# A fused attention and two-layer MLP kernel: block 1 from f32 to three f16 passes, with the elementwise work dealt out anew among VectorE, ScalarE and GpSimd

## The chip, the cores and the metric

One core of a Trainium2 chip. The metric is the device time of one execution in microseconds (us), the median of several executions; lower is better. The engines are named PE (TensorE), DVE (VectorE), ACT (ScalarE), POOL (GpSimd) and SP (SyncE, which issues the DMAs here).

## The reference

Inputs are f32 for q, k, v, p and f64 bits for the weights, decoded to f32 on the chip. Sizes: 8 batches, 8 heads, 576 tokens each, head size 64, 32 packed rows; 4608 tokens in all.

```python
def sm_attn(qq, kk, vv):            # softmax(qq kk^T / 8) vv
    ...
p_packed = sm_attn(p, k, v)         # 32 rows per head
x = sm_attn(q, p_packed, p_packed)  # (4608, 512) after the heads are joined
# first layer: d_ff 2048
h = x @ w_in
P = a[0] + a[1]*h + a[2]*h**2 + a[3]*h**3
Q = 1.0 + abs(b[0])*abs(h) + abs(b[1])*h**2
x = (P / (Q + 1e-06)) @ w_out
# second layer: d_ff 1024
h = x @ w_in2
solu = h * softmax(h)
ln = (solu - mean(solu)) / sqrt(var(solu) + 1e-06) * g_ln
out = ln @ w_out2
```

## The kernel before

Tokens go through in 9 blocks (index j) of 512. `attention(b)` makes the packed rows of batch b: scores (`a_s1`), transposes (`a_tr`), product with v (`a_pp`), a transpose and a maximum (`a_pt`), and `a_pw`, which multiplies the packed rows by `w_in`, so that the first layer's matmul takes the attention weights of a block straight to h. `a_s2` makes the attention weights of block j on DVE (a chain of 1024-column instructions) into the tile `at`.

A block has 16 tiles i of 128 rows of d_ff by 512 tokens. `m_h` makes h of one tile on PE; `elem` turns it into the ratio g; `m_y` multiplies g by four slices of `w_out` and adds into four PSUM banks. After tile 15, `y_out` copies the sum to `ybig`, and the second layer follows in four groups of 128 tokens: `s_h2` (PE), `s_sm` (maximum, exp, product), `s_lt` (halves and a DMA transpose into `lbig`), `s_ln` (a chain of small POOL instructions) and `s_out` (PE, then a copy and the output DMA).

A matmul is either f32, or three f16 passes of operands split into a high and a low half (high by high, high by low, low by high). `NRAW` says how many leading blocks and batches stay f32: with `NRAW = 2`, blocks 0 and 1 have f32 g and f32 `w_out` in `m_y`, and batches 0 and 1 have f32 `pw` and f32 attention weights in `m_h`. From then on `w_split(1, c)` has replaced chunk c of f32 `w_out` (w2) by its two halves, in place and one slot further down, so that split c+1 overwrites the slot that split c read. Splitting needs a scale (`wst`, from the maximum over all of that weight); `a_pw` halves need `bnd` (from a bound over the columns of `w_in`), and the scaled coefficients of `elem` need the chain `a_scale` (tile `cf`, some 27 small steps, and `asc` for the attention weights).

`elem` of one tile before: ACT takes |h| to u; POOL makes s = (b1 u + b0) u in two instructions (L691 through the helper at L335, and L692); ACT and DVE make the numerator B; ACT takes 1/Q as exp(-ln) (L696, L697); DVE makes one correction step and the product (L698, L699, L701 or L703); from block 2 on ACT casts the high half of g (L704) and POOL subtracts for the low half (L705). u, s and B have three buffers each, h two PSUM banks, g three.

At the start all weights are loaded and decoded by DVE (`w_decode`, L399 to L401, 24 groups of 256 rows by 512 or so), through stages that lie in the places of later weights.

The order on each engine is fixed ahead by `Plan.order`: a list scheduler with a cost in ns for each part, which takes for a free engine the ready part with the smallest due time. A due time is 16 j + an offset from the table `DUE` (one for each kind of part, or one for (block, kind)) + the tile's index; a part isn't taken while its due time is more than `DUE["ahead"]` beyond PE's present tile. Each engine then runs its list in order and waits on semaphores.

## Time and profile before

| | |
|---|---|
| median of 3 executions | 1197.74 us (1196.11 to 1203.66) |
| the profiled execution, its own time | 1202.27 us |
| its span, first to last instruction | 1200.4 us |
| PE busy | 1115.8 us, 93% |
| DVE busy | 976.8 us, 81% |
| ACT busy | 762.0 us, 63% |
| POOL busy | 706.3 us, 59% |

The span is cut by the copies that end each block's sum (L728). Block 0's begins at 194.6 us, block 1's at 327.3, block 2's at 450.0 and block 8's at 1148.8; times within the span are in us from its start. A busy share is the union of an engine's instructions; PE's contains the filling and draining of its pipeline.

### The profile page before, as it was taken

The page shows a single profiled execution, that of the slowest core. Times are in us where ns is not written, and L with a number is a line of the kernel's source. Part 1 is how long each engine was busy: PE and PEld are TensorE (multiplying, and loading weights), DVE is VectorE, ACT ScalarE, POOL GpSimd, SP SyncE. Part 2 cuts the span into 40 slices and gives each one's busy share as a digit, 9 for nine tenths or more (in the row PEclk, how much of TensorE's full clock was granted, in tenths as well). Part 3 has the DMA queues.
Part 4 walks back from the last instruction along what each step waited for, and adds up shares of the span by engine and source line. Part 5 has one row for each costly group of instructions (what it writes and reads, how often), then busy time and mean ns, then how long its engine had stood idle before and what let it go on. Part 6 is the DMA issues. An engine that isn't in the chain of part 4 may idle for free.

```text
span 1200.4 us, 17951 instructions
## 1 busy us (share of the span) xinstructions
PE 1115.8 (93%) x6549; PEld 529.7 (44%) x6550; DVE 976.8 (81%) x1477; ACT 762.0 (63%) x1256; POOL 706.3 (59%) x931
## 2 busy tenths in 40 slices
PE   4678989999999999999999998999999999999998
PEld 1133344444444454444544454444444444444443
DVE  5987999999978978888878887888788886788633
ACT  3556666676856667567756766577656666667624
POOL 0163847554658647676666655765675865867612
PEclk9698999999999999999999999999999999999999
DMA  9664033110222121311231114111311121211123
GB/s 342 224 230 161 7 123 99 36 53 1 54 77 67 27 54 55 88 27 28 62 109 27 27 40 131 27 27 27 117 28 27 27 53 28 53 27 27 27 53 88
DMA packets 108120, 83.54 MB, mean 70 GB/s; under 512 B 78208, under 2 KB 88576, under 8 KB 108032
## 3 DMA queue, kind: packets, MB, share of 16 engines
q1 hardware_dynamic: 108032, 82.40, 24.4%
q8 instruction: 51, 0.84, 0.3%
q14 instruction: 37, 0.30, 0.1%
HBM read 54.07 MB, written 9.44 MB: 53 GB/s over the span
## 4 chain that ended last, share of the span: by engine, by line
PE 47%; DVE 23%; POOL 13%; ACT 9%; issue 5%; DMA 2%; SPq 0%; DVEq 0%; ACTq 0%; POOLq 0%
PE P L329 37%; PE h L329 9%; POOL s L692 4%; POOL cf L335 3%; DVE B L699 3%; POOL s L335 2%; DVE s L698 2%; POOL g L705 2%; ACT u L696 2%; DVE B L694 2%; DVE B L695 2%; POOL d L335 1%; DVE w L401 1%; DMA lbig<-lbig 1%; DVE at L629 1%
## 5 line engine op out<-in xcount | busy, mean ns | idle before, releaser
L329 PE MATMUL P<-g,w 128*128 128x512 f16 (+1 forms) x1600 | 423.4, 414 | 0.7 <-DVE ybig L729 0.7
L329 PE MATMUL h<-at,pw 128*128 128x192 f16 (+11 forms) x1408 | 235.4, 315 | 8.3 <-ACT at L646 3.2
L335 POOL TENSOR_SCALAR s<-u,aba 128x512 f32<-128x512 f32 x130 | 137.6, 1058 | 173.7 <-ACT u L690 150.9
L329 PEld LDWEIGHTS <-w 128*128 128x128 f16 x1440 | 138.4, 98 | 167.5 <-issue 12.1
L329 PE MATMUL P<-w,ybig 128*128 128x512 f16 x864 | 193.9, 381 | 9.0 <-DVE pw L539 2.5
L705 POOL TENSOR_TENSOR g<-B,g 128x512 f16<-128x512 f32 x112 | 144.2, 1287 | 80.9 <-ACT g L704 76.6
L692 POOL TENSOR_TENSOR s<-s,u 128x512 f32<-128x512 f32 x130 | 186.3, 1433 | 7.0
L329 PE MATMUL P<-w,lbig 128*128 128x512 f16 x768 | 173.0, 379 | 4.9 <-DVE pw L539 2.9
L335 POOL TENSOR_SCALAR d<-d 128x1 f32<-128x1 f32 x216 | 85.3, 395 | 156.6 <-ACT E L790 73.1
L696 ACT ACTIVATE u<-s,lnb 128x512 f32<-128x512 f32 x130 | 93.8, 721 | 98.4 <-POOL s L692 97.9
L698 DVE SCALAR_TENSOR_TENSOR s<-s,u 128x512 f32<-128x512 f32 x130 | 109.2, 840 | 47.8 <-ACT u L697 47.0
L329 PEld LDWEIGHTS <-ybig 128*128 128x128 f16 x864 | 84.7, 98 | 114.2 <-issue 16.0
L329 PEld LDWEIGHTS <-pw 128*128 128x128 f16 x1152 | 101.6, 98 | 64.5 <-issue 13.3
L329 PEld LDWEIGHTS <-lbig 128*128 128x128 f16 x768 | 74.6, 98 | 92.6 <-issue 8.1
L694 DVE SCALAR_TENSOR_TENSOR B<-h,cf,B 128x512 f32<-128x512 f32 x112 | 83.0, 741 | 27.5 <-ACT B L693 27.3
L693 ACT ACTIVATE B<-h,cf 128x512 f32<-128x512 f32 x112 | 86.6, 773 | 21.5 <-POOL g L705 21.5
L699 DVE SCALAR_TENSOR_TENSOR B<-B,cf,u 128x512 f32<-128x512 f32 x101 | 98.2, 972 | 0.0
L697 ACT ACTIVATE u<-u,lnb 128x512 f32<-128x512 f32 x133 | 95.6, 719 | 2.0
L690 ACT ACTIVATE u<-h,cf 128x512 f32<-128x512 f32 x101 | 68.9, 682 | 39.9 <-PE h L329 38.1
L695 DVE SCALAR_TENSOR_TENSOR B<-B,cf,h 128x512 f32<-128x512 f32 x112 | 82.8, 739 | 1.5
L704 ACT CAST g<-B 128x512 f16<-128x512 f32 x112 | 68.6, 613 | 21.6 <-PE P L329 16.9
L703 DVE SCALAR_TENSOR_TENSOR B<-s,B 128x512 f32<-128x512 f32 x98 | 81.0, 827 | 1.1
(144 smaller groups left out, 1469.3 us busy)
## 6 DMA issues: line engine op xcount, KB each, us to landing
w<-in_w_in_dram SPq DMA_DIRECT2D x10, 1024.0 KB, 9.2
kq<-in_kT_dram SPq DMA_DIRECT2D x8, 1152.0 KB, 6.2
w<-in_w_out_dram SPq DMA_DIRECT2D x9, 1024.0 KB, 8.1
kq<-in_qT_dram SPq DMA_DIRECT2D x9, 1024.0 KB, 5.4
out_dram<-w SPq DMA_DIRECT2D x36, 256.0 KB, 2.4
v<-in_vN_dram SPq DMA_DIRECT2D x15, 512.0 KB, 3.7
lbig<-in_w_out_dram SPq DMA_DIRECT2D x3, 1024.0 KB, 5.4
lbig<-in_w_in_dram SPq DMA_DIRECT2D x2, 1024.0 KB, 7.0
```

What stands on the lines that cost most here:

```text
L329: nc.tensor.matmul(out=o, lhsT=lhsT, rhs=rhs, start=start, stop=stop)
L335: gp.tensor_scalar(out=o, in0=i, scalar1=s1, scalar2=s2, op0=o0, **({"op1": o1} if o1 else {}))
L692: pool(due, c_pool(512, 2), lambda: gp.tensor_tensor(out=T(s_), in0=T(s_), in1=T(u_), op=ALU.mult), [u_, s_], [s_])
L693: sc(due, c_act(512, 163), lambda: act.activation(out=T(B_), in_=T(h_), func=AF.Identity, scale=coef(17), bias=coef(16)), [h_, *R], [B_], ...
L694: dve(due, c_dve(512), lambda: stt(out=T(B_), in0=T(h_), scalar=coef(14), in1=T(B_), op0=ALU.mult, op1=ALU.mult), [h_, B_, *R], [B_])
L695: dve(due, c_dve(512), lambda: stt(out=T(B_), in0=T(B_), scalar=coef(15), in1=T(h_), op0=ALU.subtract, op1=ALU.mult), [h_, B_, *R], [B_])
L696: sc(due, c_act(512, 105), lambda: act.activation(out=T(u_), in_=T(s_), func=AF.Ln, scale=2.0 ** -40, bias=lnb[:, 0:1]), [s_, "lnb"], [u_])
L697: sc(due, c_act(512, 105), lambda: act.activation(out=T(u_), in_=T(u_), func=AF.Exp, scale=-1.0, bias=lnb[:, 1:2]), [u_, "lnb"], [u_])
L698: dve(due, c_dve(512, 140), lambda: stt(out=T(s_), in0=T(s_), scalar=1.0 + 1e-6, in1=T(u_), op0=ALU.add, op1=ALU.mult), [s_, u_], [s_])
L699: dve(due, c_dve(512, 240), lambda: stt(out=T(B_), in0=T(B_), scalar=coef(18), in1=T(u_), op0=ALU.subtract, op1=ALU.mult), [B_, u_, *R], [B_])
L703: dve(due, c_dve(512, 95), lambda: stt(out=T(B_), in0=T(s_), scalar=2.0, in1=T(B_), op0=ALU.subtract, op1=ALU.mult), [s_, B_], [B_])
L705: pool(due, (1250, 1290), lambda: gp.tensor_tensor(out=T(g_)[:, 1, :], in0=T(B_), in1=T(g_)[:, 0, :], op=ALU.subtract), [B_, g_], [g_])
```

## The change

- `NRAW` goes from 2 to 1: block 1 takes g and `w_out` as f16 halves, and batch 1 takes `pw` and attention weights as f16 halves (448 of block 1's 512 tokens and 128 of block 2's; the 64 tokens of batch 0 in block 1 stay f32). `w_split(1, c)` now stands among block 0's tiles.
- For `w_out`, the low half no longer comes from one DVE instruction: ACT scales the f32 chunk in place, and POOL subtracts the high half.
- In block 0, and on the even tiles of later blocks, s comes from ACT (Square, and Abs with a new coefficient) and one DVE instruction; POOL keeps the odd tiles of blocks 1 to 8.
- `a_scale` has one more small POOL step.
- The planner gets other costs, a rule that it starts no part marked `port` while another such part or a POOL part is under way in its model, and a new table of due times, with offsets for each weight group and for blocks 0, 1 and 8.

```diff
-    NRAW = 2
+    NRAW = 1
+    LOW_POOL = {1: 1, 2: 0, 3: 0}
+    Q_POOL = lambda j, i: j > 0 and i % 2
+    LO_POOL = lambda j, i: True
...
+        if port or eng == "POOL":
+            self.port.add(n)
...
+                        if n in self.port and port_at > now:
+                            held.append((due, n))
+                            continue
...
+                    if got in self.port:
+                        port_at = now + occ
...
-        lat = (2.4 * n + 220) if tensors > 1 else (1.3 * n + 330)
+        lat = (2.14 * n + 175) if tensors > 1 else (0.94 * n + 290)
...
+        if LOW_POOL[w]:
+            sc(due, c_act(512, 100), lambda: act.activation(out=raw[w][:, c + 1, :], in_=raw[w][:, c + 1, :], func=AF.Copy, scale=s), [b, ("wst", w), a], [b])
+            pool(due, (1117, 1157), lambda: gp.tensor_tensor(out=spl[w][:, c, 1, :], in0=raw[w][:, c + 1, :], in1=spl[w][:, c, 0, :], op=ALU.subtract), [a, b], [a, ("spl", w, c)])
+            return
...
+                      ("p", C(22), C(14), abc[:, 4:5], None, ALU.mult),
...
-        sc(due, c_act(512, 65), lambda: act.activation(out=T(u_), in_=T(h_), func=AF.Abs, scale=coef(14)), [h_, *R], [u_], [(u_, "u"), (s_, "s")])
-        pool(due, c_pool(512), lambda: ps_(T(s_), T(u_), aba[:, 5:6], aba[:, 4:5], ALU.mult, ALU.add), [u_, "ab"], [s_])
-        pool(due, c_pool(512, 2), lambda: gp.tensor_tensor(out=T(s_), in0=T(s_), in1=T(u_), op=ALU.mult), [u_, s_], [s_])
+        if Q_POOL(j, i):
+            sc(due, c_act(512, 65), lambda: act.activation(out=T(u_), in_=T(h_), func=AF.Abs, scale=coef(14)), [h_, *R], [u_], [(u_, "u"), (s_, "s")])
+            pool(due, c_pool(512), lambda: ps_(T(s_), T(u_), aba[:, 5:6], aba[:, 4:5], ALU.mult, ALU.add), [u_, "ab"], [s_])
+            pool(due, c_pool(512, 2), lambda: gp.tensor_tensor(out=T(s_), in0=T(s_), in1=T(u_), op=ALU.mult), [u_, s_], [s_])
+        else:
+            sc(due, c_act(512, 65), lambda: act.activation(out=T(s_), in_=T(h_), func=AF.Square, scale=coef(14)), [h_, *R], [s_], [(s_, "s")])
+            sc(due, c_act(512, 65), lambda: act.activation(out=T(u_), in_=T(h_), func=AF.Abs, scale=coef(22)), [h_, *R], [u_], [(u_, "u")])
+            dve(due, c_dve(512), lambda: stt(out=T(s_), in0=T(s_), scalar=aba[:, 5:6], in1=T(u_), op0=ALU.mult, op1=ALU.add), [u_, s_, "ab"], [s_], port=True)
...
```

## Rows read from the trace of the kernel before

**Rows 1.** The page's first part: busy time of each engine in us (its share of the span) and its instructions.

```profile
PE 1115.8 (93%) x6549; PEld 529.7 (44%) x6550; DVE 976.8 (81%) x1477; ACT 762.0 (63%) x1256; POOL 706.3 (59%) x931
```

**Rows 2.** Busy time by stretches: the stretch, its length, then busy us (instructions) of PE, PEld, DVE, ACT, POOL, the granted share of PE's clock, the DMA engines' share, GB/s.

```profile
0.00:60.00 60.00, 31.28 (x245) 11.59 (x249) 45.69 (x64) 27.96 (x56) 5.07 (x8) 0.80 0.80 283
60.00:83.60 23.60, 23.14 (x115) 9.22 (x108) 20.77 (x31) 16.28 (x29) 13.27 (x6) 1.00 0.79 292
83.60:93.10 9.50, 0.00 (x0) 0.01 (x1) 4.73 (x6) 3.40 (x6) 5.95 (x2) 0.67 0.00 0
93.10:194.60 101.50, 94.44 (x494) 40.09 (x494) 93.82 (x148) 64.06 (x119) 59.72 (x67) 0.96 0.32 104
194.60:327.30 132.70, 129.14 (x512) 61.01 (x511) 127.52 (x195) 93.92 (x158) 73.90 (x92) 1.00 0.15 41
327.30:450.00 122.70, 118.85 (x782) 59.53 (x781) 101.09 (x154) 78.63 (x126) 78.86 (x109) 1.00 0.23 55
450.00:1148.80 698.80, 671.03 (x4190) 326.78 (x4189) 563.16 (x845) 456.36 (x735) 461.17 (x617) 1.00 0.19 48
```

**Rows 3.** The page's chain of work that ended last, its shares of the span by engine.

```profile
PE 47%; DVE 23%; POOL 13%; ACT 9%; issue 5%; DMA 2%; SPq 0%; DVEq 0%; ACTq 0%; POOLq 0%
```

**Rows 4.** PE's instructions grouped by line, tiles and shape over the span: count, busy us, mean ns of one record, idle before. An f32 matmul leaves two records, an f16 pass one.

```profile
L329 PE MATMUL P<-g,w 128*128 128x512 f16 x1344 | 307.8, 379 | 0.2 <-DVE ybig L729 0.2
...
L329 PE MATMUL P<-g,w 128*128 128x512 f32 x256 | 115.7, 598 | 0.5 <-DVE ybig L729 0.5
...
L329 PE MATMUL h<-at,pw 128*128 128x448 f32 x64 | 27.6, 553 | 0.0
...
L329 PE MATMUL h<-at,pw 128*128 128x448 f16 x96 | 20.8, 353 | 0.4 <-DVE B L695 0.4
...
L329 PE MATMUL h<-at,pw 128*128 128x128 f32 x64 | 10.1, 281 | 0.0
...
L329 PE MATMUL h<-at,pw 128*128 128x128 f16 x96 | 8.0, 219 | 0.0
```

**Rows 5.** Instructions in order of time around 83 us, from POOL's, PE's and DVE's timelines: start, us, engine, line, operation, tiles, count, and idle time before it with what ended it.

```profile
77.41 10.88 POOL L335 TENSOR_SCALAR s<-u,aba 128x512 f32<-128x512 f32 x1 [3.73 <-DVE g L701]
...
93.13 0.59 PE L329 MATMUL P<-w,ones 128*32 128x512 bf16 x1 [9.54 <-ACT pw L534]
...
77.16 1.21 DVE L401 SCALAR_TENSOR_TENSOR w<-w,w 128x1024 uint32<-128x1024 uint32 x1
...
96.35 0.28 DVE L332 TENSOR_SCALAR p<-P,sum 128x64 f32<-128x64 f32 x1 [8.02 <-PE P L329]
```

**Rows 6.** DVE's groups between 60 and 450 us: count, busy us, mean ns, idle before.

```profile
L698 DVE SCALAR_TENSOR_TENSOR s<-s,u 128x512 f32<-128x512 f32 x50 | 37.6, 753 | 5.1 <-ACT u L697 4.9
L699 DVE SCALAR_TENSOR_TENSOR B<-B,abc,u 128x512 f32<-128x512 f32 x32 | 29.1, 910 | 0.0
L458 DVE SCALAR_TENSOR_TENSOR w<-w,wst 128x512 f16<-128x512 f32 x32 | 26.8, 843 | 0.0
...
L699 DVE SCALAR_TENSOR_TENSOR B<-B,cf,u 128x512 f32<-128x512 f32 x18 | 17.9, 995 | 0.0
L703 DVE SCALAR_TENSOR_TENSOR B<-s,B 128x512 f32<-128x512 f32 x18 | 16.1, 893 | 0.2
...
L539 DVE SCALAR_TENSOR_TENSOR pw<-P,bnd,pw 128x1024 f16<-128x1024 f32 x8 | 10.2, 1276 | 1.7 <-ACT pw L538 1.7
```

**Rows 7.** Three DVE lines over the span: count, duration of one in ns (least/median/most), first and last start. h lies in PSUM; s, u and B lie in SBUF.

```profile
L698 DVE SCALAR_TENSOR_TENSOR s<-s,u x130: 643/692/3035, 64.3 to 1133.6; 128x512 f32<-128x512 f32 x130
...
L694 DVE SCALAR_TENSOR_TENSOR B<-h,cf,B x112: 707/740/753, 303.3 to 1136.2; 128x512 f32<-128x512 f32 x112
...
L699 DVE SCALAR_TENSOR_TENSOR B<-B,cf,u x101: 734/746/1760, 305.4 to 1139.3; 128x512 f32<-128x512 f32 x101
```

**Rows 8.** POOL's groups between 60 and 450 us, the same columns as rows 6.

```profile
L692 POOL TENSOR_TENSOR s<-s,u 128x512 f32<-128x512 f32 x50 | 75.0, 1499 | 3.2
L335 POOL TENSOR_SCALAR s<-u,aba 128x512 f32<-128x512 f32 x49 | 65.3, 1332 | 80.3 <-ACT u L690 59.5 <-DVE g L701 18.6 <-ACT d L793 1.3
L705 POOL TENSOR_TENSOR g<-B,g 128x512 f16<-128x512 f32 x18 | 23.3, 1297 | 12.1 <-ACT g L704 12.0
```

**Rows 9.** ACT's groups between 60 and 450 us, the same columns.

```profile
L457 ACT ACTIVATE w<-w,wst 128x512 f16<-128x512 f32 x32 | 22.7, 715 | 10.2 <-DVE w L458 5.1 <-DVE w L452 3.9 <-POOL wst L335 1.1
...
L690 ACT ACTIVATE u<-h,cf 128x512 f32<-128x512 f32 x19 | 12.9, 680 | 4.6 <-PE h L329 4.5
L704 ACT CAST g<-B 128x512 f16<-128x512 f32 x18 | 11.0, 610 | 3.7 <-DVE B L703 2.5 <-PE P L329 1.2
```

**Rows 10.** In order of time: the first and last part of block 0's `cf` chain on POOL, the copy that ends block 1's attention weights on ACT, and the first h matmuls of block 1 on PE.

```profile
122.72 0.92 POOL L335 TENSOR_SCALAR cf<-pmx 128x1 f32<-128x1 f32 x2
...
134.15 1.59 POOL L335 TENSOR_SCALAR cf<-cf 128x1 f32<-128x1 f32 x2
...
138.51 1.12 ACT L646 COPY at<-E 128x128 f32<-128x128 f32 x2
...
156.38 2.12 PE L329 MATMUL h<-at,pw 128*128 128x64 f32 x8
```

**Rows 11.** What PE waited for between 450 and 1200 us: us in total, times, longest.

```profile
PE P L329 <- DVE E L757: 5.7, 4, 2.8
PE P L518 <- DVE p L332: 5.3, 4, 1.6
```

More of the change, by code (lines that the diff above doesn't have):

```diff
@@ L50, in __init__, with add @@
         self.parts, self.last_w, self.readers, self.users, self.kind, self.place = [], {}, {}, {}, {}, {}
-        self.slots, self.held, self.pace = {}, {}, {}
+        self.slots, self.held, self.pace, self.port = {}, {}, {}, set()
     def hold(self, key, slot):
         self.kind[key], self.held[key] = None, slot
-    def add(self, eng, due, cost, fn, r=(), w=(), new=(), pace=None):
+    def add(self, eng, due, cost, fn, r=(), w=(), new=(), pace=None, port=False):
         n = len(self.parts)
+        if port or eng == "POOL":
+            self.port.add(n)
         if pace is not None:
@@ L100, in order @@
                 heapq.heappush(ready[p[0]], (p[1], n))
-        out, now, events, pace = [], 0.0, [], 0.0
+        out, now, events, pace, port_at = [], 0.0, [], 0.0, 0.0
         bytes_free = 0.0
@@ L314, in pe, with dve @@
         plan.add("PE", due, c_pe(mms), run, r, w, new, pace)
-    def dve(due, cost, fn, r=(), w=(), new=()):
-        plan.add("DVE", due, cost, fn, r, w, new)
+    def dve(due, cost, fn, r=(), w=(), new=(), port=False):
+        plan.add("DVE", due, cost, fn, r, w, new, port=port)
     def sc(due, cost, fn, r=(), w=(), new=()):
@@ L856, in fused_kernel @@
         for g in range(4):
-            w_load(w, g, at(0, f"L{w}", g), places.get((w, g), lstage))
-            w_decode(w, g, at(0, f"D{w}", g))
+            w_load(w, g, at(0, f"L{w}{g}"), places.get((w, g), lstage))
+            w_decode(w, g, at(0, f"D{w}{g}"))
     w_bound(at(0, "bound"))
```

37 lines of the change are left out of this document (20 added, 17 removed), and 20 rows, old and new, of the table DUE.

## The prediction, made before the change was run

> **What bounds the kernel now.** I read the busy shares first, then the stretches, then the chain. PE is busy 93% of the span, DVE 81%, ACT 63%, POOL 59% [rows 1]: PE leaves some 85 us, and less PE work can shorten the kernel only where nothing else is full too. The stretches say where that is [rows 2]. From 194.6 to 327.3, which is most of block 1, PE is busy 129.1 of 132.7 us, and DVE 127.5: both are full. In blocks 2 to 8, as far as they show (327.3 to 1148.8), PE has 790 of 821.5 us and DVE 664, so there DVE has room. The chain that ended last is only 47% PE, with 23% DVE and 13% POOL [rows 3], so the order of DVE's and POOL's work counts where PE is not packed. One hole stands out: 83.6 to 93.1 us, with no PE work at all [rows 2]. Behind it is one POOL instruction of a tile's s, 10.88 us long from 77.41 [rows 5], where the two POOL steps of a tile take 1.33 and 1.50 us in the mean [rows 8]. DVE ran from before it until 88.33 (96.35 less 8.02 idle) [rows 5]; POOL came through when DVE stopped. ACT, which needs s, stood, and PE waited 9.54 us for a copy queued behind it on ACT.
>
> **What PE saves.** A record count gives one f32 matmul as two records. The f32 product with w_out takes 115.7 us for blocks 0 and 1, so 57.9 for one block; three f16 passes take 307.8 us for seven blocks, 44.0 for one: 13.9 us less in block 1 [rows 4]. The 448-token piece of h goes from 27.6 to 20.8, the 128-token piece in block 2 from 10.1 to 8.0 [rows 4]: 6.8 and 2.1. Together 22.8 us. The 64 tokens of batch 0 in block 1 save nothing.
>
> **What leaving POOL saves.** Block 0 has no large POOL step on its denominators any more, so the wait of rows 5 has no place there. That is 9.5 us of PE's time, and 1.5 to 4 us of slow clock (granted share 0.67 in the hole, 0.96 in the 101.5 us after it [rows 2], 4% of 101.5 at most); I take 1.8, as the rest of that stretch has waits of its own: 11.3 us. DVE gets back its 8.0 us of that idle time.
>
> **What DVE takes on, 60 to 450 us.** Its busy time is 20.8 + 4.7 + 93.8 + 127.5 + 101.1 = 347.9 of 390 us [rows 2]. Added: the new instruction that makes s, on 16 tiles of block 0, 8 of block 1 and the 9 of block 2 and its successor that fall in here, 33 times. The trace has none; the nearest is L698, same operands, s and u in SBUF: median 0.692, mean 0.753 here [rows 6, 7]. I take 0.692, 22.8 us (24.8 at the mean). Four low halves of batch 1's `pw` at 1.276 are 5.1 us [rows 6]; the low halves of its attention weights, about a 1024-column step, 1.2 more by the same row. Gone: 16 low halves of w_out at 0.843, 13.5 us [rows 6]. Net +15.6.
>
> Against that stands relief. Instructions with both inputs in SBUF run up to 3.04 us (L698) or 1.76 (L699) against medians near 0.7, while L694, which reads h from PSUM, never exceeds 0.753 [rows 7]: the former collide with POOL. Over the medians of rows 7 the excess between 60 and 450 us is 50 x 0.061 (L698), 32 x 0.164 and 18 x 0.249 (L699), 18 x 0.201 (L703, against L698's median) and 32 x 0.097 (L458, against L699's): 19.5 us [rows 6, 7]. POOL's large steps there cost (75.0 + 65.3)/50 = 2.8 us a tile [rows 8]; 33 tiles less are 92, and 16 subtractions for w_out and 16 for block 1's g at 1.30 [rows 8] bring 42 back, so POOL falls from 231.7 us [rows 2] by 51, 22%. By that share relief is 4 us; the ends are 0 (the new steps collide as much as the old) and 19.5 (none is left). I take 5. DVE's work becomes 347.9 + 15.6 - 5 = 358.5 us.
>
> The Trainium skill ("SBUF — State Buffer", Who interferes with whom) says that a DVE instruction with two SBUF inputs and a GpSimd instruction reading SBUF exclude each other, and the second to issue blocks until the first finishes. L694 against L698 agrees; the 10.88 us doesn't, since the POOL step outlasted some nine DVE instructions. By the rule it would have waited one, 1.2 us; the hole would then have another cause and could stay, and the sum below would be about 9 us less gain. The measurement decides.
>
> **What that leaves, 60 to 450 us.** PE alone could save 22.8 + 11.3 = 34 us there. DVE can't follow: 358.5 us of work in 390 - 34 = 356. In its densest stretch DVE reached 127.5/132.7, 96% [rows 2]. At that density 358.5 us take 373, a gain of 17 us; with no relief 378 (12), with all of it 358 (32). If DVE keeps all its idle time but the hole, it is 358.5 + 42.1 - 8.0 = 392.6: nothing. I take 17, since DVE's idle time outside the hole is mostly waiting for PE and ACT, which also get work earlier when PE is ahead.
>
> **Blocks 3 to 8.** DVE gets some 47 more such instructions, 33 us, on 563 of 699 us [rows 2]; POOL loses 47 x 2.8 = 130 of 461, so collisions fall by a quarter to a third. PE's waits there are for DVE's queue (5.7, 5.3 us and smaller) [rows 11], 28 us in all by rows 2. The two effects on DVE pull apart; I take a gain of 2, with -6 (slower) and +10 as ends.
>
> **What I cost at nothing.** ACT: 33 more passes at up to 0.68, 16 at 0.715 for w_out, 16 casts at 0.61 [rows 9], 44 us on 256 of 390 [rows 2]; 300 of 373 fits. But if all of w_out's 16 splits fall in 93 to 194.6 us, ACT has 64.1 + 22.9 + about 8 of 101.5 there: the cover is thin. A split costs 0.715 + 0.715 + 1.30, 2.7 us in series, so each one that slips behind its product costs up to that; block 1's products come 7 to 8 us apart (132.7/16 less what goes), so they don't wait for long. New waits: block 1's attention weights now need the `cf` chain of block 1, 12 to 13 us on POOL for block 0's, ending at 135.7 [rows 10], and w_out's scale; block 1's weights were ready at 139.6 and first used at 156.4 [rows 10], 17 us of cover. Queued behind that wait on DVE would be the decoding of the second layer's weights and block 0's tiles. If the chain for block 1 follows that of block 0, it ends near 149, and the rest (two DVE steps, copies, some 5 us) at 154: just in time; each us later is a us of PE. The extra `a_scale` step, 8 times under half a us on POOL, is beside other work. SP's DMAs are the same ones, in a new order; before 60 us PE is idle 28.7 us [rows 2], which I leave as it is, with +-4 us for a start that goes otherwise.
>
> **The sum.** 17 + 2 = 19 us. The profiled execution took 1202.27 us, 1.87 more than its span, and would take 1183.3. It lies 4.5 above the median of three, and the differences are what I trust, so from 1197.74: **1179 us**.
>
> **The rivals.**
> - PE stays the bound: DVE's collisions go almost entirely (19.5 us of relief), and later blocks lose a third of their waits. For it: the planner now keeps such parts apart, and DVE has room after block 2. Against it: its times are a model's, and DVE would have to run at over 95% for 350 us. Gain 34 + 8 = 42, 1156; halfway, 1166.
> - DVE eats the gain: it keeps the idle time it has outside the hole (34 us), the stretch lasts 388 to 393. For it: it is 96% busy in block 1 already. 1190 to 1200.
> - The starved POOL step comes back elsewhere: the subtractions for w_out read SBUF in just the time when DVE is fullest, and splits, ACT and PE queue behind them. 9.5 us of the gain go: 1188. (By the Trainium skill's rule above the time would come out there as well, with the hole left where it is.)
> - Slower: the added DVE instructions collide with the new POOL subtractions at 0.84 each (what L458 costs now [rows 6]), no relief, and the first block's tiles then wait for DVE: 33 x 0.84 + 6.3 - 13.5 = 20.5 us on top of 347.9, with all 42.1 idle: 410 against 390, and PE's saving lies idle. It decides once DVE's net addition exceeds the idle time it gives back (8 us). About +12 with some of the idle used: 1210.
> - The change doesn't do what it says (the f16 passes don't come at 44 us a block because their halves arrive late): as the second rival.
>
> **How the numbers follow.** Forecast (1168 to 1187) 0.42; PE-bound (1152 to 1168) 0.20; DVE eats it 0.20; starved step 0.08; slower 0.10. 1% of the median, 12 us, is about what a measurement here tells from no change. Faster than 1186: 0.40 + 0.20 = 0.60. Within 1%: 0.30. Slower: 0.10. The range leaves out the slower case and the best half of the PE-bound one: 1160 to 1200.
>
> **What would show it.** After: f16 products only from block 1 on, and PE busy about 1093 us; no POOL step over 3 us before 100 us and no PE gap near 9 us there; block 1's stretch at 113 to 120 us with DVE above 93% in it, block 0's end within 8 us of 194.6. L698 and L699 nearer to their medians would show relief. The prediction is wrong if DVE is well below 93% in blocks 0 and 1 while PE still waits (then the order is at fault), if the first 60 us move by more than 4 us, or if blocks 3 to 8 shorten by more than 10.

## The result, and the profile after

After the change the kernel takes 1155.51 us (median of 4 runs, 1155.43 to 1161.18) against 1200.2 us for the kernel before on the same chip (median of 4, 1196.11 to 1203.66): a ratio of 0.9641, 95% interval 0.9594 to 0.9687. The forecast was 1179, with 1160 to 1200 as its range. The direction was right, the size was not: some 45 us instead of 19, and the time lies below the range. The profiled execution of after took 1155.43 us with a span of 1153.7, that of before 1202.27 with 1200.4.

Busy time of each engine, and the engines' shares of the chain that ended last, from the page of after; they answer to [rows 1] and [rows 3]:

```profile
PE 1090.7 (95%) x6678; PEld 520.8 (45%) x6678; DVE 968.7 (84%) x1552; ACT 811.5 (70%) x1368; POOL 586.1 (51%) x824
...
PE 66%; DVE 10%; ACT 9%; issue 2%; POOL 0%; ACTq 0%
```

PE's work fell by 25.1 us. The span fell by 46.7, so PE's idle time fell by 21.6. POOL, 13% of the chain before, is at 0% in it.

The same stretches as in [rows 2], cut at the same copies, which now begin at 196.1, 309.7, 427.2 and 1101.7 us, and then 60 us to the end of block 2 in one (columns as there):

```profile
0.00:60.00 60.00, 29.28 (x229) 9.97 (x230) 45.05 (x63) 28.28 (x56) 0.19 (x4) 0.83 0.86 300
60.00:196.10 136.10, 121.29 (x619) 52.89 (x619) 130.67 (x210) 114.95 (x206) 56.90 (x71) 0.92 0.33 115
196.10:309.70 113.60, 104.88 (x569) 48.95 (x568) 105.32 (x167) 81.99 (x136) 68.13 (x85) 0.98 0.21 54
309.70:427.20 117.50, 116.31 (x813) 57.95 (x811) 107.86 (x178) 91.47 (x152) 70.69 (x97) 1.00 0.23 57
427.20:1101.70 674.50, 671.03 (x4233) 329.46 (x4232) 560.09 (x900) 473.80 (x787) 380.85 (x537) 1.00 0.20 50
...
60.00:427.20 367.20, 342.47 (x1997) 159.78 (x1998) 343.85 (x553) 288.41 (x492) 195.72 (x252) 0.97 0.26 78
```

Two things are to be seen. From 60 us to the end of block 2 the kernel is 22.8 us shorter (390.0 to 367.2), with DVE busy 94% of it; the forecast had 17. In blocks 3 to 8 it is 24.3 us shorter (698.8 to 674.5), where the forecast had 2. PE's busy time there is the same to 0.1 us (671.0), so all of that is waiting that went: PE idles 3.5 us of 674.5, before 27.8 of 698.8. What is left of the rows that answer to [rows 11], PE's waits between 427.2 and 1101.7 us:

```profile
PE P L545 <- DVE p L355: 1.5, 4, 0.4
PE P L381 <- ACT ppT L546: 1.4, 4, 0.4
PE h L352 <- DVE B L728: 0.5, 1, 0.5
```

Why DVE had time for its added instructions shows in its groups in blocks 3 to 8 (count, busy us, mean ns, idle before). First before, then after; L698, L699 and L703 are L731, L732 and L736 now, and L725 is the new instruction:

```profile
L699 DVE SCALAR_TENSOR_TENSOR B<-B,cf,u 128x512 f32<-128x512 f32 x83 | 80.3, 968 | 0.0
L698 DVE SCALAR_TENSOR_TENSOR s<-s,u 128x512 f32<-128x512 f32 x80 | 71.6, 894 | 42.6 <-ACT u L697 42.1 <-POOL g L705 0.4
...
L703 DVE SCALAR_TENSOR_TENSOR B<-s,B 128x512 f32<-128x512 f32 x80 | 65.0, 812 | 0.9
```

```profile
L732 DVE SCALAR_TENSOR_TENSOR B<-B,cf,u 128x512 f32<-128x512 f32 x86 | 68.6, 798 | 0.0
L731 DVE SCALAR_TENSOR_TENSOR s<-s,u 128x512 f32<-128x512 f32 x75 | 58.6, 782 | 10.7 <-ACT u L730 8.7 <-POOL g L739 2.0
L736 DVE SCALAR_TENSOR_TENSOR B<-s,B 128x512 f32<-128x512 f32 x76 | 56.1, 738 | 0.6
L725 DVE SCALAR_TENSOR_TENSOR s<-s,aba,u 128x512 f32<-128x512 f32 x37 | 28.2, 761 | 2.8 <-ACT u L724 2.8
```

All four have both inputs in SBUF. The means fell by 74 to 170 ns towards the medians near 0.7 us [rows 7], and so DVE did the added instructions in no more time than before: 560.1 us against 563.2 [rows 2].

Block 0 is the odd one. The hole of [rows 5] is gone: between 60 and 110 us PE's longest wait is 2.2 us, and POOL has no large step before 97.88 us. Still the block's sum is copied at 196.1 us instead of 194.6. PE's last f32 product of block 0 ends at 174.22, where before it ended at 193.43. PE then makes h for block 1's tiles and packed rows of a later batch, but block 1's products need the PSUM banks that hold block 0's sum, and their first comes at 200.85, just behind the first copies to `ybig`. In order of time (start, us, instruction, idle before): block 0's last products on PE, two POOL steps on `cf` that bring in the second layer's scale, ACT's copies and block 1's first products on PE; then the stretch between the two products in the columns of [rows 2]; then the two products in before:

```profile
171.48 2.74 PE L352 MATMUL P<-g,w 128*128 128x512 f32 x6
...
192.03 0.68 POOL L358 TENSOR_SCALAR cf<-cf,wst 128x1 f32<-128x1 f32 x1
...
193.54 0.22 POOL L358 TENSOR_SCALAR cf<-cf 128x1 f32<-128x1 f32 x1
...
196.14 2.10 ACT L764 ACTIVATE ybig<-P,cf 128x1024 f16<-128x1024 f32 x2
...
200.85 5.34 PE L352 MATMUL P<-g,w 128*128 128x512 f16 x24 [0.85 <-DVE ybig L765]
...
174.20:200.90 26.70, 16.80 (x194) 9.23 (x193) 23.25 (x43) 21.41 (x40) 13.80 (x16) 0.74 0.19 63
```

```profile
189.83 3.60 PE L329 MATMUL P<-g,w 128*128 128x512 f32 x8
...
197.11 2.41 PE L329 MATMUL P<-g,w 128*128 128x512 f32 x5 [0.48 <-DVE ybig L729]
```

In the program the copy stands behind the chain `a_scale2`, whose first two steps are those on POOL; ACT is not idle right before it. PE idles 9.9 us of the 26.7, in waits of up to 2.4 us for DVE and ACT, and its granted clock is 0.74 in the mean, between its two levels. Before, the two products lay 3.7 us apart, with 0.5 us of idle time. So new waits, together as long as the old hole, stand at the end of block 0. The copy's time is no measure of PE's work on block 0, and the sum to the end of block 2 is the better one.

### The profile page after: what moved, and what is told of

Read it like the earlier page. It is cut to its first block, busy times and chain, and to the rows that moved or that the text cites. A ratio compares the mean times of both kernels' runs of the same rounds, so it can differ in the third digit from the quotient of the medians.

```text
span 1153.7 us, 18175 instructions
## 1 busy us (share of the span) xinstructions
PE 1090.7 (95%) x6678; PEld 520.8 (45%) x6678; DVE 968.7 (84%) x1552; ACT 811.5 (70%) x1368; POOL 586.1 (51%) x824
## 4 chain that ended last, share of the span: by engine, by line
PE 66%; DVE 10%; ACT 9%; issue 2%; POOL 0%; ACTq 0%
PE P L352 52%; PE h L352 13%; DVE B L732 2%; DVE s L731 1%; ACT B L726 1%; DVE B L727 1%; ACT u L729 1%; ACT u L730 1%; DVE w L485 1%; ACT g L737 1%; DVE B L736 1%; ACT E L826 1%; ACT E L517 1%; DVE B L728 1%; ACT u L724 1%
## 5 line engine op out<-in xcount | busy, mean ns | idle before, releaser
L352 PEld LDWEIGHTS <-w 128*128 128x128 f16 x1632 | 156.9, 98 | 191.9 <-issue 16.1
L739 POOL TENSOR_TENSOR g<-B,g 128x512 f16<-128x512 f32 x128 | 171.1, 1338 | 123.4 <-ACT g L737 120.1
L352 PE MATMUL h<-at,pw 128*128 128x448 f16 (+8 forms) x1472 | 228.5, 304 | 5.2 <-DVE B L728 3.5
L358 POOL TENSOR_SCALAR d<-d 128x1 f32<-128x1 f32 x216 | 113.9, 528 | 173.0 <-ACT E L788 57.2
L352 PEld LDWEIGHTS <-pw 128*128 128x128 f16 x1344 | 117.3, 99 | 74.5 <-issue 14.3
L726 ACT ACTIVATE B<-h,cf 128x512 f32<-128x512 f32 x128 | 99.6, 779 | 1.9 <-POOL cf L358 1.2
L731 DVE SCALAR_TENSOR_TENSOR s<-s,u 128x512 f32<-128x512 f32 x115 | 88.5, 769 | 14.3 <-ACT u L730 12.1
L732 DVE SCALAR_TENSOR_TENSOR B<-B,cf,u 128x512 f32<-128x512 f32 x117 | 92.5, 791 | 0.0
L786 DVE TENSOR_REDUCE d<-P 128x1 f32<-128x1024 f32 x36 | 43.9, 1219 | 55.9 <-PE P L352 55.9
L719 ACT ACTIVATE u<-h,cf 128x512 f32<-128x512 f32 x56 | 38.4, 685 | 71.9 <-PE h L352 64.9
L358 POOL TENSOR_SCALAR s<-u,aba 128x512 f32<-128x512 f32 x50 | 45.0, 900 | 64.4 <-ACT u L719 64.2
L736 DVE SCALAR_TENSOR_TENSOR B<-s,B 128x512 f32<-128x512 f32 x103 | 74.7, 725 | 0.6
```

What stands on the lines that cost most here:

```text
L352: nc.tensor.matmul(out=o, lhsT=lhsT, rhs=rhs, start=start, stop=stop)
L358: gp.tensor_scalar(out=o, in0=i, scalar1=s1, scalar2=s2, op0=o0, **({"op1": o1} if o1 else {}))
L726: sc(due, c_act(512, 163), lambda: act.activation(out=T(B_), in_=T(h_), func=AF.Identity, scale=coef(17), bias=coef(16)), [h_, *R], [B_], ...
L731: dve(due, c_dve(512, 0), lambda: stt(out=T(s_), in0=T(s_), scalar=1.0 + 1e-6, in1=T(u_), op0=ALU.add, op1=ALU.mult), [s_, u_], [s_], port ...
L732: dve(due, c_dve(512), lambda: stt(out=T(B_), in0=T(B_), scalar=coef(18), in1=T(u_), op0=ALU.subtract, op1=ALU.mult), [B_, u_, *R], [B_], ...
L736: dve(due, c_dve(512, 0), lambda: stt(out=T(B_), in0=T(s_), scalar=2.0, in1=T(B_), op0=ALU.subtract, op1=ALU.mult), [s_, B_], [B_], port=True)
```

## The experiments

All lengths below are us of the profiled execution, cut at the same copies. "Excess" is DVE's time in blocks 3 to 8 above the lower quartile, over the whole kernel, of each instruction's own line and shape. I take it for what its instructions took longer than they do undisturbed; where instructions overlap, not all of it is busy time. A stretch with the same work in the same order comes out the same within 2 us: blocks 3 to 8 take 698.6 to 700.4 in before, e10 and e18, and 674.4 to 675.3 in after, e9, e11 and e16.

| kernel | time | ratio to before (95%) | block 0 | 1 | 2 | 3 to 8 | DVE, POOL busy in 3 to 8 | excess |
|---|---|---|---|---|---|---|---|---|
| before | 1198.5 to 1203.5 | | 194.6 | 132.7 | 122.7 | 698.8 | 563.1, 461.2 | 71.6 |
| after | 1155.5 | 0.964 (0.959, 0.969) | 196.1 | 113.6 | 117.5 | 674.5 | 560.1, 380.8 | 31.6 |
| e1 | 1185.0 | 0.988 (0.985, 0.991) | 200.0 | 116.7 | 126.7 | 688.3 | 575.0, 491.0 | 74.4 |
| e2 | 1188.7 | 0.991 (0.988, 0.994) | 190.2 | 134.0 | 122.7 | 690.6 | 567.6, 352.2 | 45.2 |
| e19 | 1179.3 | 0.980 (0.976, 0.984) | 194.3 | 132.7 | 122.8 | 676.1 | 535.6, 358.7 | 43.6 |
| e17 | 1178.1 | 0.981 (0.976, 0.986) | 197.6 | 114.5 | 118.3 | 693.3 | 605.0, 392.0 | 47.0 |
| e4 | 1187.0 | 0.990 (0.987, 0.993) | 200.7 | 130.3 | 119.0 | 683.7 | 546.8, 467.6 | 48.3 |
| e6 | 1238.7 | 1.028 (1.026, 1.030) | 193.9 | 143.6 | 122.8 | 725.6 | 550.3, 474.7 | 54.4 |
| e13 | 1181.8 | 0.984 (0.980, 0.988) | 187.2 | 112.6 | 128.6 | 699.2 | 571.5, 366.4 | 40.9 |
| e3 | 1232.5 | 1.027 (1.024, 1.031) | 196.2 | 144.1 | 118.2 | 723.1 | 579.2, 383.9 | 49.1 |
| e5 | 1247.7 | 1.036 (1.034, 1.037) | 233.0 | 108.5 | 124.5 | 727.7 | 564.8, 466.9 | 63.5 |
| e7 | 1202.8 | 1.000 (0.998, 1.002) | 174.6 | 145.7 | 134.0 | 695.3 | 564.9, 382.0 | 37.5 |
| e9 | 1167.0 | 0.971 (0.969, 0.973) | 206.1 | 114.6 | 118.7 | 674.6 | 559.9, 379.4 | 31.7 |
| e10 | 1205.1 | 1.001 (0.999, 1.003) | 194.3 | 132.8 | 124.2 | 700.4 | 562.0, 461.0 | 70.7 |
| e11 | 1171.4 | 0.975 (0.973, 0.977) | 198.2 | 124.6 | 119.7 | 674.4 | 559.8, 380.0 | 31.2 |
| e16 | 1164.3 | 0.969 (0.965, 0.973) | 201.0 | 115.7 | 117.5 | 675.3 | 560.1, 379.2 | 32.2 |
| e18 | 1202.7 | 1.001 (0.999, 1.003) | 194.4 | 132.7 | 122.9 | 698.6 | 559.7, 461.2 | 67.9 |

### The later blocks: the move or the order

**e1_back_on_pool**, after's order of work, with the even tiles of blocks 1 to 8 handed back to POOL:

```diff
-            dve(due, c_dve(512), lambda: stt(out=T(s_), in0=T(s_), scalar=aba[:, 5:6], in1=T(u_), op0=ALU.mult, op1=ALU.add), [u_, s_, "ab"], [s_], port=True)
...
+                    ps_(T(s_), T(u_), aba[:, 5:6], aba[:, 4:5], ALU.mult, ALU.add)
+                    gp.tensor_tensor(out=T(s_), in0=T(s_), in1=T(u_), op=ALU.mult)
```

> The kernel after, with its order kept as it is, but the even tiles of blocks 1 to 8 have their denominators on POOL again: ACT's Square goes, ACT's Abs takes the old coefficient, and POOL's two steps stand where the DVE instruction stood. Theory M (the move off POOL gave blocks 3 to 8 their 24 us): collisions and the longer chain are back, +15 to +25 us, 1171 to 1181. Theory O (the order gave it: the planner's rule and due times): 0 to +6 us, 1155 to 1162.

**e2_half_off**, the reverse: before's order, denominators dealt out as after:

```diff
+        on_pool = j > 0 and i % 2
...
+            if not on_pool:
+                act.activation(out=T(s_), in_=T(h_), func=AF.Square, scale=coef(14))
```

> The kernel before, with its order kept as it is, but block 0's and the even tiles' denominators on ACT and DVE: Square beside Abs on ACT, one DVE instruction where POOL's first step stood, nothing where its second stood. The factor of b0 is left out of the even tiles' Abs, which has no cost. Theory M: the hole at 83 us goes and blocks 3 to 8 lose most of their 28 us of PE waits, 1168 to 1180. Theory O: only the hole goes, at most 10 us, 1188 to 1198.

e1 came out at 1185.0, above the range of either theory: of its loss against after 14 us lie in blocks 3 to 8, but 16 in blocks 0 to 2. e2's 1188.7 is in the range of Theory O, though 8 us of its gain are in blocks 3 to 8. With before and after these are a square of order and place. Blocks 3 to 8: old order 698.8 on POOL and 690.6 halved; new order 688.3 and 674.5. The move is worth 8 us in the old order and 14 in the new, the order 10 and 16. Neither alone gives the 24.

**e19_less_pool_on_before**, before's order, with less of POOL's work and nothing more for DVE:

```diff
-        pool(due, c_pool(512, 2), lambda: gp.tensor_tensor(out=T(s_), in0=T(s_), in1=T(u_), op=ALU.mult), [u_, s_], [s_])
+        pool(due, c_pool(512, 2), lambda m=64 if j >= 3 else 512: gp.tensor_tensor(out=T(s_)[:, 0:m], in0=T(s_)[:, 0:m], in1=T(u_)[:, 0:m], op=ALU.mult), [u_, s_], [s_])
```

> The kernel before in its own order, with the second GpSimd step of the denominators (s times u) cut to 64 of its 512 columns in blocks 3 to 8; the other columns' factor u is left out. VectorE and ScalarE have the same work. Theory (in before's later blocks what TensorE waits for goes back to tiles whose chains stand behind GpSimd, and to VectorE's collisions with it; it falls with GpSimd's time): blocks 3 to 8 with the tail 15 us or more shorter than before's 750, 1180 to 1187. Rival (the order itself makes those waits, whoever computes s, as the halves moved in the old order gained only 6 to 8 us there): under 10 us shorter, 1193 to 1201.

**e17_more_dve_late**, after's order, one more DVE instruction on the even tiles of blocks 3 to 8:

```diff
+                if j >= 3:
+                    stt(out=T(s_), in0=T(s_), scalar=1.0, in1=T(s_), op0=ALU.mult, op1=ALU.max)
```

> After's order, with one more 512-column two-input VectorE instruction of no effect ahead of the s instruction on the even tiles of blocks 3 to 8: 47 instructions, some 33 us of VectorE's time, about 6 us a block. Theory (in after's later blocks TensorE is the pace and VectorE, with 98 of 116 us, has room): within 5 us of 1155.5. Rival (VectorE's work or its collisions set the pace there, so that the fall in collisions is itself the gain of 24 us): 1175 or more. In between, with 2 to 3 us a block as in e1_back_on_pool: 1165 to 1175, latency of the chain of a tile rather than VectorE's sum.

The later blocks of e2, e19 and e17, in the columns of [rows 2]:

```profile
446.90:1137.50 690.60, 669.32 (x4193) 326.88 (x4191) 567.64 (x890) 480.51 (x781) 352.24 (x527) 1.00 0.20 48
```

```profile
449.80:1125.90 676.10, 667.85 (x4189) 326.35 (x4188) 535.59 (x845) 458.35 (x734) 358.65 (x617) 1.00 0.20 50
```

```profile
430.40:1123.70 693.30, 675.29 (x4231) 329.06 (x4230) 604.96 (x946) 475.78 (x788) 391.95 (x537) 1.00 0.19 48
```

The cleaner pair is after and e17, where ACT's time differs by 2 us and POOL's by 11: 44.9 us more of DVE, 18.8 us longer, 0.42 us of time for 1 us of DVE. The rival named for e17 (1175 or more) came. My theory, that DVE has room in the later blocks because it is busy 98 of 116 us, falls: some 40% of what is added comes out, even at 83%. Whether by DVE's sum or by the longer chain of a tile, e17 doesn't tell. e2 and e19 have the same order and nearly the same POOL time (352 and 359 us); DVE has 32.0 us less in e19 and the stretch is 14.5 us shorter, 0.45. But ACT also has 22 us less there (its Square passes are not in e19), and POOL's step in a tile's chain is shorter, so this ratio may be too high. From before to e2, POOL has 109 us less, DVE 4.5 more and ACT 24 more, for a gain of 8.2: with DVE taken at 0.45 and ACT at nothing, 0.1 us for 1 us of POOL. e19's own theory came, with blocks 3 to 8 shorter by 22.7 us (15 or more expected). PE's new waits in e17 are for DVE's next tile:

```profile
PE h L352 <- DVE B L732: 7.1, 7, 1.8
PE P L352 <- DVE pw L566: 3.2, 4, 0.9
```

At these prices (a linear estimate from three pairs) the change's 80 us less of POOL and 3 us less of DVE are worth 8 + 1 = 9 of the 24 us in blocks 3 to 8; 15 are left for the order. From before to e1 the same sum gives 8 us slower, measured was 10 faster: 18 for the order. The two agree, but both are what a sum leaves over. They don't say what in the order shortens PE's waits.

### The rule, the costs and the table of due times

**e4_rule_on_before** is before's work planned with the new costs and the `port` rule and the old due times; **e6_costs_on_before** is the same without the rule; **e13_rule_half_on_before** is e4 with the denominators dealt out as after.

```diff
-        if port or eng == "POOL":
+        if False:                            # e6
...
-    Q_POOL = lambda j, i: True
+    Q_POOL = lambda j, i: j > 0 and i % 2    # e13
```

> The work of the kernel before (two f32 blocks, all denominators on POOL, low halves of w_out on DVE) with the new planner costs and its port rule, but the old table of due times. Theory M: within 6 us of the kernel before, 1192 to 1205. Theory O with the rule as its main part: 12 to 25 us faster, 1175 to 1188; with the due times as its main part, within 6 us as well.

> As e4_rule_on_before (the work and the table of the kernel before, the planner's new costs), but without the port rule. If the rule made that run's 12 us, this one is back at 1194 to 1206; if the costs made them (POOL steps cheaper, no allowance for collisions in DVE's), 1183 to 1190.

> Two f32 blocks as before, with the new costs, the port rule and the old table of due times, and the denominators dealt out as after the change; it differs from e4_rule_on_before (1187.0) by the denominators alone, and from after by the f16 block, w_out's low halves and the table. Theory (move and order do it together, as the fixed orders had it: the move is worth 8 us in the old order and 23 in the new): 1164 to 1179, and blocks 3 to 8 with the tail near 731. Rival (the due times written for this distribution carry it): within 6 us of e4, 1181 to 1193. Rival (the move hurts without its own table): above 1193.

The rule alone, between e6 and e4, is worth 52 us (46 by the ratios) and most of it in blocks 1 and 3 to 8; but the new costs without it lose some 35 us, which no expectation had, so it is not to be read as a gain on before, which is 1.0% for both together. The excess fell in each: 71.6 us before, 54.4 with the new costs alone (e6), 48.3 with costs and rule (e4), 45.2 with half the tiles off POOL (e2), 40.9 with costs, rule and half the tiles (e13), 31.6 in after. So 17 of e4's 23 us are there without the rule, and the rule's 52 us are hardly a matter of collisions (6 us of excess against 42 us of time in blocks 3 to 8). Nor does the excess by itself set the length of blocks 3 to 8: e1 has 74.4, as much as before, and is 10 us faster there; e13 has 40.9 and takes 699.2, as long as before. Fewer collisions explain how DVE found time for its added instructions; what the order is worth beside that, they don't explain. e13 is only 5 us faster than e4 (7 by the ratios), where the fixed orders had promised 8 to 14 in blocks 3 to 8 alone: the rival (due times written for this distribution carry it) was right. In e13 the gain is in blocks 0 to 2 (428.5 against 450.1) and the later blocks give 15 back. The rule with the old costs was not run.

**e3_rule_early** (after replanned, rule only in the first 150 us of the plan), **e5_one_raw_on_before** (before with `NRAW = 1` alone) and **e7_y_first** (after replanned with `a_scale2` behind `y_out`):

```diff
+                        if n in self.port and port_at > now and now < 150e3:   # e3
...
+    NRAW = 1                                                                   # e5
```

> The kernel after, planned anew with the rule that keeps port parts apart dropped from 150 us of the plan's own time on, everything else as it is. Theory M: the time hardly moves, 1153 to 1161. Theory O, with the rule as its main part: blocks 3 to 8 get their waits back, +10 to +20, 1166 to 1176; with the due times as its main part, 0 to +5.

> The kernel before with one f32 block in place of two and nothing else: old planner, old table, all denominators on POOL, low halves of w_out on DVE. If PE bounds block 1, as the second part of the result suggests, the 22.8 us of PE work come through: 1174 to 1180. If DVE bounds blocks 0 and 1, as the forecast had it, the low halves and POOL's collisions eat most of it: 1188 to 1200.

> The kernel after with one thing moved in the program: the chain that puts the second layer's scale into the block's coefficients (a_scale2) stands behind y_out, which then no longer waits for it. In the kernel after, block 0's product ends at 174 us and its copy starts at 196, behind that chain. If that wait holds PE up: 5 to 12 us faster, 1144 to 1151. If DVE, 95% busy there, sets the pace: within 4 us, 1151 to 1160.

All three are over 45 us slower than after. e7 gets block 0's output 21 us earlier and loses 32 in block 1, 16 in block 2 and 21 in blocks 3 to 8. A table of due times fits the parts and costs for which it was made, so a part tried alone with a new plan is priced by its plan and not by itself. I draw no price from e3, e5 and e7; the comparisons in a fixed order carry the argument.

### What sets the pace in the first blocks

**e10_less_pe_on_before** cuts a quarter of the columns of block 1's products in before's order; **e11_four_passes** adds a fourth f16 pass to block 1 and batch 1 in after's.

```diff
+                m = 384 if j == 1 else 512                        # e10, and n * 3 // 4 for batch 1's h
...
+            passes = (*PASS, (1, 1)) if j == 1 else PASS          # e11
```

> The kernel before, with its order kept; batch 1's h matmuls and block 1's f32 product take only three quarters of their columns, which leaves out that quarter of the result and costs PE what three f16 passes would (about 20 us less in block 1, 2 less in block 2). Everything else as before. If DVE sets the pace in block 1, as the forecast had it: block 1 shorter by at most 5 us, 1192 to 1200. If PE does: shorter by 14 to 20, 1178 to 1186.

> The kernel after, with its order kept; block 1's product and batch 1's h take a fourth f16 pass (low by low), which costs PE about what f32 did: 64 x 0.22 + 32 x 0.19 + 32 x 0.06 = 22 us more. If DVE sets the pace in block 1 of the kernel after: at most 8 us slower, 1156 to 1164. If PE does: 16 to 22 us, 1171 to 1178.

e10's block 1, in the columns of [rows 2]:

```profile
194.60:327.30 132.70, 118.06 (x525) 62.70 (x524) 127.82 (x195) 93.78 (x157) 71.72 (x92) 0.96 0.15 41
```

PE is busy 11 us less than in [rows 2] (some 20 were meant), the stretch takes the same 132.7 us, and DVE's 127.8 are its pace: less PE work by itself is worth nothing in the old kernel. In after's order some 20 us more PE work (busy 1110.5 against 1090.7) cost 15.8 us by the medians and 14.9 in the span: there PE is the pace for three quarters of it. So less PE work pays in after's order and not in before's, and between them DVE's busy time in block 1 fell from 127.5 to 105.3 us.

**e16_low_on_dve** puts the low halves of w_out back on DVE in after's order, **e9_block0_pool** block 0's denominators back on POOL.

```diff
-            pool(due, (1117, 1157), lambda: gp.tensor_tensor(out=spl[w][:, c, 1, :], in0=raw[w][:, c + 1, :], in1=spl[w][:, c, 0, :], op=ALU.subtract), [a, b], [a, ("spl", w, c)])
+            pool(due, (1117, 1157), lambda: v_.scalar_tensor_tensor(out=spl[w][:, c, 1, :], in0=raw[w][:, c + 1, :], scalar=s, in1=spl[w][:, c, 0, :], op0=ALU.mult, op1=ALU.subtract),
+                 [a, b], [a, ("spl", w, c)])
```

> After's order, with the low halves of w_out by one VectorE instruction again at the same place (ScalarE's second pass gone, GpSimd's subtraction gone). Theory (VectorE is full up to the end of block 1, so 16 instructions at 0.75 to 0.84 us, 12 to 13.5 us, are on the path): 1161 to 1169, all of it before 430 us. Rival (it was as well hidden there, as e9 priced block 0's denominators alone): within 3 us of 1155.5. Rival (the freed ScalarE and GpSimd time helps more): under 1152.

> The kernel after, with its order kept, but block 0's 16 denominators on POOL again (its two steps stand where the DVE instruction stood, ACT's Square goes). If the forecast's reading of the hole is right, a POOL step is held up for several us behind DVE's decoding rows in the first 100 us, and block 0 ends 5 to 15 us later: 1160 to 1170. If the hole was tied to the old order's row of instructions alone: 0 to 4 us, 1155 to 1160.

e16 is 8.8 us slower than after by the medians (7.3 by the span) and e9 11.5 (12.0); nearly all of both is in blocks 0 and 1 (316.7 and 320.8 against 309.7). For e16 the ground was that 12 to 13.5 us of DVE are on the path there; some two thirds of that came out, with ACT's second pass and POOL's subtraction gone beside it. e9's time is in the range of its theory, but not for the theory's reason: its longest large POOL step before the end of block 0 takes 2.8 us, so its loss is not a hole.

### The hole in block 0

**e18_hole_tile** was to take the long POOL step alone out of before's order (`here = j == 0 and i == 3`).

> The kernel before in its own order, with one tile changed: block 0's fourth, whose GpSimd step took 10.88 us, gets its s from ScalarE and one VectorE instruction (its Abs keeps the old coefficient, so the factor of |h| is left out in this tile). Theory (the step starved behind the row of overlapping VectorE instructions, and the hole is its whole price): no GpSimd step over 3 us and no TensorE wait near 9 us before 100 us, block 0 shorter by 5 to 11 us, the kernel at 1190 to 1198 against 1202. Rival (the row was there in any case and something else fills the time): a wait of over 5 us of TensorE still in 75 to 100 us, block 0 within 2 us of 194.6. Rival (the hole goes and the rest of block 0 is full, as after's block 0 suggests): no such wait, block 0 still shorter by under 4 us.

It missed: the tile changed was the one ahead. Its two POOL steps are gone and the next one is as it was; PE still waits 9.5 us, and the kernel takes the same time. POOL's step, and PE's wait from 60 to 195 us:

```profile
77.18 10.87 POOL L335 TENSOR_SCALAR s<-u,aba 128x512 f32<-128x512 f32 x1 [6.00 <-DVE g L717]
...
PE P L329 <- ACT pw L534: 9.5, 1, 9.5
```

So the length does not come from the steps ahead of it in POOL's queue. Three other kernels put one 512-column POOL step that reads SBUF beside test rows of DVE instructions: **e8_starve** and **e12_rows** with rows that mostly write one tile again and again, so that each instruction waits for the last, **e14_apart** with rows whose outputs alternate between two tiles, so that the next begins before the last has ended, as in the hole (0.60 or 1.13 us from start to start with durations of 0.68 and 1.21).

The lines are e14's:

```diff
+                ps_(q_, m_, aba[:, 5:6], aba[:, 4:5], ALU.mult, ALU.add)      # the POOL step
+                for k, f in enumerate(row):
+                    f(outs[1 + k % 2 if apart else 1])                        # the row on DVE
```

> The kernel after with a test section at its end, which adds about 110 us and whose time is not compared. Eight times, POOL gets one 512-column step that is ready when a row of DVE instructions begins: 12 of 1024 columns with both inputs in SBUF, 12 with one input in PSUM, 20 one-input shifts at double rate, and 12 two-input ones with one from PSUM after each four; all twice. If a POOL step can be passed over by DVE for as long as DVE has such instructions in a row, it takes the whole row with both inputs in SBUF (about 14 us), 0.8 us beside the PSUM ones, and about 5 us with a PSUM one after four. If it waits for one instruction only, it takes at most 2 us in all of them. Beside the shifts: the whole row (13 us) by the first, 1.5 by the second.

> The kernel after with a second test section at its end (its time is not compared), POOL's step of 512 columns with its two pointer scalars, ready when a row of DVE instructions begins. Rows: the row that stood beside the 10.88 us (decoding steps of both kinds and 512-column two-input steps mixed), the two two-input decoding steps in turn, the one-input decoding step alone, the three decoding steps in turn, and 512-column two-input steps alone; all twice. If that row starves POOL: over 8 us in the first and fourth, under 2 in the others. If it doesn't: under 2.5 us in all, and the 10.88 us came from something else.

> After, with test rows of VectorE instructions added in front, each row beside one 512-column GpSimd step that reads SBUF: twelve two-input 1024-column instructions whose outputs alternate between two tiles (so that they overlap), the same twelve all into one tile (each waits for the last), eighteen 512-column ones alternating, eighteen one-input shifts alternating, and a row mixed as in the hole. The whole time means nothing. Theory (a row of overlapping instructions keeps GpSimd out until the row ends, as the 10.88 us step suggested): over 8 us in the alternating rows, under 2 us in the dependent row. Rival (GpSimd waits for one instruction at most, as the Trainium skill, 'SBUF — State Buffer', section Who interferes with whom, has it): under 2.5 us in every row, and the 10.88 us stay open.

e8's steps took 0.62 to 1.62 us and e12's 1.14 to 1.77. The steps of e14, start and duration, by row: twelve two-input instructions of 1024 columns into one tile; eighteen two-input ones of 512 alternating; eighteen one-input shifts of 1024 alternating; a mixed row alternating; the twelve two-input ones alternating; and the shifts again:

```profile
1158.22 1.67 POOL L358 TENSOR_SCALAR kq<-lbig,aba 128x512 f32<-128x512 f32 x1 [0.56 <-DVE lbig L355]
1174.00 2.18 POOL L358 TENSOR_SCALAR kq<-lbig,aba 128x512 f32<-128x512 f32 x1 [14.11 <-DVE lbig L355]
1185.59 11.38 POOL L358 TENSOR_SCALAR kq<-lbig,aba 128x512 f32<-128x512 f32 x1 [9.40 <-DVE lbig L355]
1197.53 2.71 POOL L358 TENSOR_SCALAR kq<-lbig,aba 128x512 f32<-128x512 f32 x1 [0.56 <-DVE lbig L355]
1208.70 14.17 POOL L358 TENSOR_SCALAR kq<-lbig,aba 128x512 f32<-128x512 f32 x1 [8.46 <-DVE lbig L355]
...
1250.79 11.38 POOL L358 TENSOR_SCALAR kq<-lbig,aba 128x512 f32<-128x512 f32 x1 [9.40 <-DVE lbig L355]
```

Two instructions of the twelve alternating ones, the second beginning before the first has ended:

```profile
1208.53 1.21 DVE L942 SCALAR_TENSOR_TENSOR ybig<-w 128x1024 f32<-128x1024 f32 x1
1209.66 1.21 DVE L942 SCALAR_TENSOR_TENSOR lbig<-w 128x1024 f32<-128x1024 f32 x1
```

A POOL step can be kept out for a whole row: eighteen shifts of 0.60 are 10.8 us and the step took 11.38; twelve of 1.13 are 13.6 and it took 14.17. The same twelve instructions, each waiting for the last, let it through in 1.67. The theory holds for two of the four overlapping rows; in the other two POOL came through after three instructions (the fourth was then 0.4 us longer), and what decides that stays open. The first pass over the twelve alternating ones is no measure of the 512-column step, since POOL still had steps of one column to do; but these came through beside that row, in 1.05 to 3.31 us each, so the row does not keep out every step:

```profile
1145.31 7.31 POOL L358 TENSOR_SCALAR d<-d 128x1 f32<-128x1 f32 x3 [0.64 <-ACT d L830]
```

The row that was mixed like the hole is one of the two that let POOL through, in 2.71 us. So that the 10.88 us have this cause is likely and not shown. For it speaks where the step ended: at 88.29 us, 0.56 behind the end of the last DVE instruction with two inputs in SBUF, while the next, which reads h from PSUM, was still running. Twelve instructions had gone by since 77.16. The last two in before:

```profile
86.52 1.21 DVE L400 SCALAR_TENSOR_TENSOR w<-w,w 128x1024 uint32<-128x1024 uint32 x1
87.65 0.67 DVE L694 SCALAR_TENSOR_TENSOR B<-h,B 128x512 f32<-128x512 f32 x1
```

The hole's price by itself stays open too, since e18 missed; e2, whose block 0 has no POOL step on denominators, ended that block 4.4 us earlier.

## Why the prediction was wrong, point by point

**PE's saving** was right: 22.8 us forecast, 25.1 measured (23.1 of it from 60 us to the end of block 2), PE busy 1090.7 against "about 1093". The product with w_out takes 351.3 us for eight blocks, 43.9 for one, as forecast.

**The hole** went as forecast. That the POOL step starved behind DVE is what e14 shows to be possible, not that it was so. The prediction read "some nine" instructions in the row and had POOL come through when DVE stopped; the trace has twelve, and POOL came through beside one that reads PSUM. What failed is the hole's worth, 11.3 us of PE's time. Up to block 0's last product it came: from 60 us to there PE idles 7.2 us, where it idled 17.0 before. It was lost behind that product: the forecast had no term for the copy of block 0's sum, and while PE waits for it 9.9 us go idle at a granted clock of 0.74. From 60 us to the end of block 2 PE's idle time is 24.7 us, where it was 24.4 with the hole in it (390.0 - 365.6, the sum of [rows 2]). No row shows the 1.8 us of slow clock that the sum added to the hole's 9.5; the clock from 60 us to the copy fell, from 0.95 to 0.92. How much of the 9.9 us another place for the copy would give back is open: e7 copied at 174.6 us, but with a new plan that lost more elsewhere.

**DVE's work from 60 us to the end of block 2.** Forecast 347.9 + 15.6 - 5 = 358.5 us; measured 343.9, so by this sum relief was 19.6 and not 5. The step that failed is "By that share relief is 4 us": I let collisions fall in proportion to POOL's busy time, 22%. They fell by half: the excess, counted in this stretch as in the table, goes from 33 to 17 us. That relief equals the forecast's upper end (19.5, "none is left") is chance, since that end counted four lines of DVE alone and 17 us are still left. Collisions go by where POOL's steps stand as well as by their sum; e4 has a third less excess in the later blocks with no less POOL work. The density was near the forecast, 94% against 96%, and with the right relief the same sum gives 344/0.96 = 358 us, against 367 measured. The forecast of 17 us there (22.8 measured) was near because a relief too small and a density too high offset each other.

**Blocks 3 to 8** are the main error: 2 us forecast with +10 as the end, 24.3 measured. The forecast's own mark for this ("if blocks 3 to 8 shorten by more than 10") was met. Two terms failed. Collisions were to fall by a quarter to a third and fell by more than half (71.6 to 31.6), so the added 33 us of DVE vanished in its own time. And the new order had no term of its own: the square of e1 and e2 puts 10 to 16 us on it. What in the order does it stays open. I had the rows for a bound, since PE's waits there were 28 us in all, and cut it to 10 for no reason in the rows; the gain was nine tenths of it.

**DVE bounds it, or PE.** The likeliest case had DVE as the bound after the change; the rival in which "PE stays the bound" with relief of 19.5 us and fewer waits later gave 1156 and is what came, at 0.20. That its total fits to 1 us is luck: 34 us in the first blocks and 8 later became 23 and 24, and collisions did not go almost entirely. e11 shows PE at the pace in after's block 1, e10 DVE in before's.

**What was right besides:** block 1 at 113.6 us (113 to 120 forecast) with DVE at 92.7% (a little under the 93% forecast), block 0's end 1.5 us later (within 8), no large POOL step before 97 us, the first 60 us within 2 us of PE's time. Beside the sum stood 9 us less gain by the rule of the Trainium skill ("SBUF — State Buffer", Who interferes with whom), with the hole left in place; the hole went.

**The low halves of w_out** were forecast to lighten DVE by 13.5 us; e16 prices them at 7 to 9.

**The parts together**, by the ratios to before times 1200 us, and only a rough sum, since each part was priced in another order: rule and costs 12 (e4), the move beside them 7 (e13), the PE work of one f16 pass's size 13 (e11), the low halves 6 (e16): 38 of 43. The new table of due times has no price of its own.

## What to carry to other kernels

Price an added DVE instruction with two SBUF inputs by where POOL's steps lie beside it, not by POOL's busy time: here half the steps (e2) or a new plan (e4) each took away a third of the collisions, both together 43% (e13) and in after 56%. But fewer collisions alone did not make the kernel faster: e13's later blocks took as long as before's. Where the chain mixes engines, PE's total waiting in a stretch is the bound on what a better order can give there; keep it as the end of the range unless a row speaks against it. An engine busy 83% of a stretch has no free room: added work there came out at about 0.42 us for 1 us, and with a schedule fixed ahead a change is only to be judged with a plan made for it. When a hole is closed, look at the end of the block for the next thing that PE waits for: here it was the copy of the sum, and it took as much.

## What the runs showed of the hardware

A row of DVE instructions that overlap can keep one POOL step waiting until the row ends: 14.17 us beside twelve and 11.38 beside eighteen in e14. The 10.88 us in the kernel before look the same, but the row mixed like that one let POOL through in 2.71 us. The Trainium skill ("SBUF — State Buffer", Who interferes with whom) lets the first to issue have the shared pair for one instruction while the other blocks. e8, e12 and the dependent row of e14 agree (0.62 to 1.77 us); the two rows above do not, and there the measurement decides: the wait went on over all of the row's instructions. Which overlapping rows let POOL in between, and why, no run here shows.
